# Score matmuls issued as four column tiles of 32 keys, in two softmax attention layers

## The chip, the cores and the metric

The kernel runs on one NeuronCore of a Trainium2 chip. The metric is the device time of one execution in microseconds. The kernel before takes 2621.23 us, the median of three runs (2619.69 to 2622.96).

Five engines run side by side and meet at semaphores: TensorE (matmuls; PE in the profile, its weight loads PEld), VectorE (DVE), ScalarE (ACT), GpSimd (POOL) and SyncE (SP, which issues transfers here). A matmul here is always a pair: a load of the stationary operand into TensorE's array, and a matmul that streams the moving operand past it into PSUM. A form such as `64*128` in the profile gives the part of the array that a pair occupies: 64 rows (the contraction) by 128 columns (the output partitions).

## The reference

Four layers follow each other, each added to its input x (2048 tokens, width 512, 32 heads of 16): softmax attention A, linear attention B, then A and B again with the same weights. The change touches only A:

```python
qkv = (x @ wqkv).reshape(B, S, 3, H, Dh)            # after a layer norm
scores = jnp.einsum("bhqd,bhkd->bhqk", q, k) * (Dh ** -0.5)
p = _softmax(scores, axis=-1)
o = jnp.einsum("bhqk,bhkd->bhqd", p, v)
return o.transpose(...).reshape(B, S, D) @ wo
```

## The kernel before

**Staging.** The heads of an A layer are taken in four octets (8 heads) of two groups (4 heads) each, g = 0 to 7. For each group two tiles `kq` of 128 partitions hold keys and queries in fp16. A head takes 64 partitions: 48 rows are the 16 dimensions in three products of high and low fp16 parts, the rest carries the softmax shift. So one `kq` tile holds two heads, one in partitions 0 to 63 (u = 0), one in 64 to 127 (u = 1).

**The loop.** Attention walks through (g, j, kt): group, block of 512 queries (4), tile of 128 keys (16), 8 x 4 x 16 = 512 steps a layer. `scores` (L807) does a step's two halves. A half takes one PSUM tile `s` of two banks (128 partitions x 2 x 512), runs one matmul for each of two heads into it (L813: stationary 64x128 keys, moving 64x512 queries), and one exponential on ScalarE (L816) from `s` to the SBUF tile `p` in float32. The pool `psS` has three such `s` tiles, `pp` has six `p` tiles. Since the two heads lie in different row halves of the array, their matmuls can run at the same time.

`pvs` (L819) does the value side two steps later (LAG = 2): for each of four heads one float32 matmul, stationary v of 128 keys x 32, moving p of 128x512, into partitions 32·hh to 32·hh + 31 of the accumulator `pv` (L831). That is the column grid `128*32`: four tiles side by side. The profile shows each float32 matmul as two load and matmul pairs, so 8 a step. After the 16th key tile `norm` (L474) turns and normalizes the result on VectorE.

**The filler.** The next octet's projections, the value projections, the output projection and the preparation of weights for B are cut into pieces; `pump` (L853) takes one piece after a step whenever a credit allows, 0.345 a step in most of the time, 0.55 once the last octet is ready. A piece of the query and key projection is 4 chunks, each as four column tiles of 32 (`mm_cols`, L549; L553), in the grid of the value matmuls; a piece of the value projection (L630) is 16 matmuls of form `128*128`; the row norms take one matmul (L653).

**Order.** In the attention loop the order on TensorE is the program's own (`manual_schedule` for PE): scores of step n, value matmuls of step n - 2, at times a piece of filler. The other engines are ordered by the framework. Between attention and the next layer lies the stage of layer B (L933 and on; its `gather`, L1060, has the matmuls of L1064).

Of the kernel before, what the change touches and what calls it, by code (L numbers as in the profile page):

```python
# [17 lines left out]
P = 128  # L18
# [25 lines left out]
def mha_hedgehog_stack(ctx, tc, x_in, a_wqkv, a_wo, b_wqkv, b_wphi, b_wo, out, shmin=SHMIN):  # L44
    nc = tc.nc
# [537 lines left out]
    class LayerA:  # L583
# [223 lines left out]
        def scores(self, g, j, kt):  # L807
            for half in range(2):
                s = psS.tile([P, 2, 512], F32, tag="S", name="s")
                for u in range(2):  # L810
                    r = 64 * u
                    t = self.kq[g][half]
                    nc.tensor.matmul(s[:, u, :], t[r:r + 64, 0, kt * P:(kt + 1) * P],  # L813
                                     t[r:r + 64, 1, j * 512:(j + 1) * 512], start=True, stop=True)
                pt = pp.tile([P, 2, 512], F32, tag="p", name="p")
                nc.scalar.activation(pt, s, AF.Exp, scale=0.25 / (QS * QS))  # L816
                self.pt[(g, j, kt, half)] = pt
# [470 lines left out]
```

## Time and profile before

| what | us |
|---|---|
| median of three runs | 2621.23 |
| the profiled execution | 2620.91 |
| its span in the profile | 2619.1 |
| first attention, first to last exponential | 84 to 1080 |
| second attention, first to last exponential | 1391 to 2364 |

Layer B and the preparation of the first layer fill the rest. How to read the lines that follow: a group line has line, engine, operation, output and inputs, form, shapes and count; then busy time, mean duration of one in ns, and the idle time of the engine just before it with what ended it. A timeline line has start (us from the start of the span), length of the merged run, engine, line, operation and count. A line of the chain has start, length, engine, what and line. TensorE's durations are from start to modelled end, so matmuls in a row overlap: the distance of two starts tells their cost.

### The profile page before, as it was taken

How to read it: one execution, taken by the hardware profiler on the slowest of the kernel's cores; microseconds unless marked ns; L12 is line 12 of the kernel's file. 1: busy time of each engine (PE TensorE's matmuls, PEld its weight loads, DVE VectorE, ACT ScalarE, POOL GpSimd, SP SyncE). 2: the span in 40 equal slices, each digit the busy share in tenths (PEclk: the TensorE clock that was granted, in tenths of full speed). 3: DMA queues.
4: the chain of work that ended last, by engine and by line, in shares of the span. 5: the costliest groups of instructions: out<-in, count | busy, mean ns of one | idle time of the engine just before them, and what ended most of it. 6: DMA issues, size and time to landing. Idle time of an engine off the chain costs nothing.

```text
span 2619.1 us, 50234 instructions
## 1 busy us (share of the span) xinstructions
PE 2503.1 (96%) x20960; PEld 812.9 (31%) x20960; DVE 997.4 (38%) x1902; ACT 2196.1 (84%) x2436; POOL 371.5 (14%) x502
## 2 busy tenths in 40 slices
PE   6899999999999899999899999999999999999998
PEld 4322222222223122355343222222222212224543
DVE  6211211221223533689872122112211302338897
ACT  5799999999899899654437999999999999994552
POOL 3000000000000000266430000000000000004552
PEclk8999999999999899999999999999999999999999
DMA  4500220130113411100234003201301230110003
GB/s 147 110 29 9 47 40 5 27 50 11 57 27 84 157 45 46 41 25 1 73 96 67 13 11 51 32 5 28 60 5 26 56 74 32 48 44 26 9 17 106
DMA packets 52414, 120.43 MB, mean 46 GB/s; under 512 B 11024, under 2 KB 14224, under 8 KB 49360
## 3 DMA queue, kind: packets, MB, share of 16 engines
q1 hardware_dynamic: 51504, 114.76, 18.3%
q8 instruction: 166, 2.72, 0.4%
q0 software_dynamic: 672, 2.36, 0.2%
q14 instruction: 72, 0.59, 0.1%
HBM read 60.06 MB, written 31.59 MB: 35 GB/s over the span
## 4 chain that ended last, share of the span: by engine, by line
PE 73%; DVE 12%; ACT 8%; issue 4%; POOL 2%; DMA 1%; ACTq 0%; SPq 0%; POOLq 0%; DVEq 0%
PE pv L831 33%; PE s L813 20%; ACT p L816 6%; PE pqk L553 5%; PE po L553 5%; DVE su L1017 2%; PE pk L946 1%; PE pbv L946 1%; PE pq L946 1%; POOL f L1026 1%; PE pst L419 1%; DVE f L1009 1%; PE pn L1086 1%; DVE su L1018 1%; DVE yt L503 1%
## 5 line engine op out<-in xcount | busy, mean ns | idle before, releaser
L816 ACT ACTIVATE p<-s 128x1024 f32<-128x1024 f32 x2048 | 1907.0, 1075 | 63.9 <-PE s L813 58.0
L831 PE MATMUL pv<-p,v 128*32 128x512 f32 x8192 | 1096.3, 607 | 13.8 <-DVE yt L476 13.7
L813 PE MATMUL s<-kq 64*128 64x512 f16 x4096 | 676.8, 384 | 23.2 <-DMA kq<-sh 2.8
L813 PEld LDWEIGHTS <-kq 64*128 64x128 f16 x4096 | 157.7, 93 | 805.6 <-issue 792.0
L831 PEld LDWEIGHTS pv<-p,v 128*32 128x32 f32 x8192 | 162.4, 108 | 370.9 <-issue 331.6
L645 POOL TENSOR_TENSOR sq<-stg 128x512 bf16<-128x512 f16 x48 | 68.9, 1435 | 1313.0 <-DVE stg L696 1306.1
L695 DVE TENSOR_SCALAR tq<-pqk,c_qk 128x512 f32<-128x512 f32 x48 | 35.1, 732 | 451.3 <-PE pqk L553 451.3
L1026 POOL TENSOR_TENSOR f<-f,su 128x1024 f32<-128x1024 f32 x62 | 120.0, 1935 | 575.7 <-DVE su L1020 547.4
L476 DVE STREAM_TRANSPOSE yt<-pv 128x512 f32<-128x512 f32 x64 | 45.8, 716 | 404.9 <-PE pv L831 404.8
L946 PEld LDWEIGHTS <-xnTa 128*128 128x128 f16 x1152 | 109.6, 98 | 139.8 <-DVE f L1010 14.8
L553 PEld LDWEIGHTS <-wA 128*32 128x32 f16 (+1 forms) x2496 | 86.4, 97 | 149.4 <-issue 100.6
L1011 ACT ACTIVATE f<-f,c_pB 128x1024 f32<-128x1024 f32 x64 | 72.5, 1148 | 38.2 <-DVE f L1010 37.9
L553 PE MATMUL pqk<-xnTb,wA 128*32 128x512 f16 (+1 forms) x1248 | 98.4, 381 | 1.1 <-ACT xnTb L429 1.1
L946 PE MATMUL pbv<-wbv,xnTa 128*128 128x512 f16 x384 | 88.2, 379 | 11.0 <-DVE f L1010 11.0
L553 PE MATMUL po<-woA,ob 128*32 128x512 f16 x1536 | 97.5, 379 | 0.0
L553 PE MATMUL pqk<-xnT,wA 128*32 128x512 f16 (+1 forms) x1224 | 92.4, 379 | 2.7 <-DVE xnT L432 2.2
L1032 ACT ACTIVATE fk<-f 128x1024 f16<-128x1024 f32 x30 | 31.7, 1057 | 74.9 <-POOL f L1026 74.9
L541 DVE SCALAR_TENSOR_TENSOR xt<-po,c_oA,xt 128x512 f32<-128x512 f32 x32 | 23.2, 724 | 183.9 <-PE po L553 183.9
L946 PE MATMUL pq<-wbqk,xnTa 128*128 128x512 f16 x384 | 88.4, 379 | 0.0
L946 PE MATMUL pk<-wbqk,xnTa 128*128 128x512 f16 x384 | 88.4, 379 | 0.0
L1058 ACT ACTIVATE qT<-pqt 128x512 f32<-128x512 f32 x64 | 34.7, 593 | 56.6 <-PE pqt L1057 56.6
L1017 DVE TENSOR_REDUCE su<-f 128x64 f32<-128x1024 f32 x64 | 77.5, 1210 | 9.7 <-ACT f L1011 8.9
(261 smaller groups left out, 1936.8 us busy)
## 6 DMA issues: line engine op xcount, KB each, us to landing
kq<-stg SPq DMA_DIRECT2D x96, 128.0 KB, 5.6
xd<-xt SPq DMA_DIRECT2D x24, 512.0 KB, 2.8
xt<-xd SPq DMA_DIRECT2D x24, 512.0 KB, 3.6
kq<-stg SPq DMA_DIRECT2D x96, 96.0 KB, 4.2
kq<-dC SPq DMA_DIRECT2D x64, 128.0 KB, 3.7
oD<-osp SPq DMA_DIRECT2D x24, 256.0 KB, 2.0
ob<-oD SPq DMA_DIRECT2D x8, 768.0 KB, 5.4
xt<-in_A_x_dram SPq DMA_DIRECT2D x8, 512.0 KB, 3.9
```

The costliest lines, as they stand in the source:

```text
L476: nc.vector.transpose(yt.rearrange("p a b -> p (a b)"), ps)
L553: nc.tensor.matmul(ps[r, :], w[:, r], x, start=(n == 0), stop=(n == 11), skip_group_check=cols)
L645: nc.gpsimd.tensor_tensor(sq, hi, hi, ALU.mult)
L695: nc.vector.tensor_scalar(tq, ps, cqk, CLAMP, op0=ALU.mult, op1=ALU.min)
L813: nc.tensor.matmul(s[:, u, :], t[r:r + 64, 0, kt * P:(kt + 1) * P], t[r:r + 64, 1, j * 512:(j + 1) * 512], start=True, stop=True)
L816: nc.scalar.activation(pt, s, AF.Exp, scale=0.25 / (QS * QS))
L831: nc.tensor.matmul(acc[32 * hh:32 * hh + 32, :], self.oct[o]["v"][:, r:r + 32], pt[:, hh % 2, :], start=(kt == 0), stop=(kt == NT - 1), sk ...
L946: nc.tensor.matmul(dst, xnT[:, a, c, t * P:(t + 1) * P], w(b, c), start=(i == 0 and c == 0), stop=(i == 2 and c == NC4 - 1))
L1011: nc.scalar.activation(f, f, AF.Exp, scale=con["pB"])
L1017: nc.vector.tensor_reduce(su, f[:, r, :], AX.X, ALU.add)
L1026: nc.gpsimd.tensor_tensor(f3, f3, self.part_sums(f3, slice(0, 64), factor), ALU.mult)
L1058: nc.scalar.activation(qT[i][:, :, t * P:(t + 1) * P], pst.rearrange("p (g t) -> p g t", g=4), AF.Copy)
```

## The change

The single score matmul of a head and key tile (64 rows x 128 keys) becomes four of 64 rows x 32 keys, each writing its 32 partitions of the same bank. The four read the same queries as moving operand. Their number goes from 4 to 16 pairs of load and matmul a step; the exponential, the value matmuls, the buffers and the filler stay as they are, and so does the order of the work. The first of the four carries the wait for a free `s` tile, and the last of a half tells ScalarE. On TensorE the program goes from 33,767 to 58,343 instructions (this includes a branch for unusual data that isn't run).

```diff
                 for u in range(2):
                     r = 64 * u
                     t = self.kq[g][half]
-                    nc.tensor.matmul(s[:, u, :], t[r:r + 64, 0, kt * P:(kt + 1) * P],
-                                     t[r:r + 64, 1, j * 512:(j + 1) * 512], start=True, stop=True)
+                    for i in range(4):
+                        k0 = kt * P + 32 * i
+                        nc.tensor.matmul(s[32 * i:32 * i + 32, u, :], t[r:r + 64, 0, k0:k0 + 32],
+                                         t[r:r + 64, 1, j * 512:(j + 1) * 512], start=True, stop=True, skip_group_check=True)
```

## The prediction

> **What bounds the kernel now.** I read the page first: the engines' totals and the chain that ended last.
>
> ```profile
> span 2619.1 us, 50234 instructions
> PE 2503.1 (96%) x20960; PEld 812.9 (31%) x20960; DVE 997.4 (38%) x1902; ACT 2196.1 (84%) x2436; POOL 371.5 (14%) x502
> PE 73%; DVE 12%; ACT 8%; issue 4%; POOL 2%; DMA 1%; ACTq 0%; SPq 0%; POOLq 0%; DVEq 0%
> PE pv L831 33%; PE s L813 20%; ACT p L816 6%; PE pqk L553 5%; PE po L553 5%; DVE su L1017 2%; PE pk L946 1%; PE pbv L946 1%; PE pq L946 1%; POOL f L1026 1%; PE pst L419 1%; DVE f L1009 1%; PE pn L1086 1%; DVE su L1018 1%; DVE yt L503 1%
> L816 ACT ACTIVATE p<-s 128x1024 f32<-128x1024 f32 x2048 | 1907.0, 1075 | 63.9 <-PE s L813 58.0
> L831 PE MATMUL pv<-p,v 128*32 128x512 f32 x8192 | 1096.3, 607 | 13.8 <-DVE yt L476 13.7
> L813 PE MATMUL s<-kq 64*128 64x512 f16 x4096 | 676.8, 384 | 23.2 <-DMA kq<-sh 2.8
> L813 PEld LDWEIGHTS <-kq 64*128 64x128 f16 x4096 | 157.7, 93 | 805.6 <-issue 792.0
> L831 PEld LDWEIGHTS pv<-p,v 128*32 128x32 f32 x8192 | 162.4, 108 | 370.9 <-issue 331.6
> L553 PEld LDWEIGHTS <-wA 128*32 128x32 f16 (+1 forms) x2496 | 86.4, 97 | 149.4 <-issue 100.6
> ```
>
> The reader sees TensorE on 73% of the chain, the value matmuls (L831) and the score matmuls (L813, the changed ones) holding 53% between them. There are 2048 exponentials, so 1024 steps of two halves (4096 score matmuls, four a step). The second view is the chain of waits inside 20 us of the first layer's attention, the third the timeline of the same stretch.
>
> ```profile
> by line: PE pv L831 49.7%; PE s L813 31.0%; PE pqk L553 13.0%; ACT p L816 5.5%; issue 1.6%; PE psn L653 1.2%; ACTq L816 0.1%
> 505.96 0.54 PE s L813 x4
> 506.50 1.00 PE pv L831 x8
> 507.50 0.54 PE s L813 x4
> 508.04 0.99 PE pv L831 x8
> 509.03 0.65 PE s L813 x4
> 509.68 0.99 PE pv L831 x8
> 510.68 0.86 PE pqk L553 x16
> 511.54 0.54 PE s L813 x4
> ```
>
> One cycle is three steps and one piece of projection: 511.54 - 505.96 = 5.58 us, all of it TensorE. ScalarE's own pace is in a timeline row where it runs four exponentials without a break:
>
> ```profile
> 205.06 3.79 ACT L816 ACTIVATE p<-s 128x1024 f32<-128x1024 f32 x4
> ```
>
> (3.79 - 1.075)/3 = 0.905 us each, so six want 5.43 us. The two engines are within 3% of each other; TensorE leads, and its only idle time in the cycle is the 0.65 in place of 0.54: 0.11 us in which the third score pair waits for ScalarE to free a bank. In the last eighth of an attention even that is gone:
>
> ```profile
> 130.00:820.00 690.00, 678.97 (x6012) 179.02 (x6010) 140.10 (x256) 674.29 (x726) 35.27 (x29) 1.00 0.18 32
> 2237.00:2364.00 127.00, 125.31 (x1194) 33.50 (x1196) 44.21 (x118) 120.27 (x129) 0.00 (x0) 1.00 0.12 41
> ```
>
> These are windows (columns: window, length, then busy time of PE, PEld, DVE, ACT, POOL, then granted clock, DMA share, GB/s). The second has 129 exponentials in 127 us, 1.97 us a step, with TensorE busy 98.7%.
>
> **The change part by part.** It removes 4 weight loads and 4 matmuls of 64x128 a step and issues 16 and 16 of 64x32: 24 more instructions a step, 24,576 in all. Bytes, banks and ScalarE's work stay. No wait is added: the first of a half's eight waits for the bank, the last one releases ScalarE. Instructions are fetched by queues of their own, the larger of them:
>
> ```profile
> q8 instruction: 166, 2.72, 0.4%
> ```
>
> Even doubled that is 0.8% of the DMA engines, and I cost it at nothing; what covers it is the engines' idle share.
>
> What could be won is the drain between column grids. The timeline shows it:
>
> ```profile
> 504.03 1.06 PE L831 MATMUL pv<-p,v 128*32 128x512 f32 x8
> 504.92 1.05 PE L553 MATMUL pqk<-xnT,wA 128*32 128x512 f16 x16
> 505.90 0.60 PE L813 MATMUL s<-kq 64*128 64x512 f16 x4
> 506.43 1.07 PE L831 MATMUL pv<-p,v 128*32 128x512 f32 x8
> 507.43 0.13 PEld L813 LDWEIGHTS <-kq 64*128 64x128 f16 x4 [0.84 <-issue]
> 507.43 0.61 PE L813 MATMUL s<-kq 64*128 64x512 f16 x4
> ```
>
> From pv to a projection in the same 128*32 grid 0.89 us go by; from pv to scores 507.43 - 506.43 = 1.00: **0.11 us lost** entering the score shape. A score pair streams twice 0.216 (0.60 less its last 0.384), yet 0.53 pass until pv: **0.10 us lost** leaving it. Both are paid in every step, 0.21 us. The first score matmul starts with its load (both rows 507.43), so the load itself isn't on the path; a 64x32 load isn't in the trace, but 64x128 takes 0.093 and 128x32 takes 0.097 to 0.108, and I cost the exchange at nothing.
>
> Does a common column grid remove them? The score tiles keep 64 rows, pv has 128. The trace has a change of rows alone, 128*128 to 64*128:
>
> ```profile
> L630 PE MATMUL pv__619<-wAv,xnT x48: 219/219/219, 51.4 to 54.1; 128*128 128x128 f16 x48
> 105.81 0.67 PE L630 MATMUL pv__1202<-wAv,xnT 128*128 128x128 f16 x9
> 106.41 0.60 PE L813 MATMUL s<-kq 64*128 64x512 f16 x4
> ```
>
> Undisturbed, these follow each other every 2.7/47 = 0.057 us; nine take 0.51, and the scores come 0.60 after the first: 0.09 us lost with the columns unchanged. So a change of rows pays the same drain, and I keep both drains: saving 0. The other bound is both gone, 0.21 a step; it is a rival below.
>
> The Trainium skill (TensorEngine Tiling (Array Packing), Key Properties) says that changing the tiling mode, not just the tile, drains TensorE, and lists 64x32 and 128x32 as different modes; by it too the saving is 0, also where this trace has no row for that very pair.
>
> What is added is the stagger. Tiles of a group start one behind the other, and a drain waits for the last. The two row tiles of a score pair start together: the x4 row is 0.60 = 0.216 + 0.384. For column tiles:
>
> ```profile
> 506.43 0.16 PEld L831 LDWEIGHTS pv<-p,v 128*32 128x32 f32 x8 [0.42 <-issue]
> 504.49 0.12 PEld L553 LDWEIGHTS <-wA 128*32 128x32 f16 x4 [0.30 <-issue]
> ```
>
> Eight loads of 0.108 lie within 0.16, so the last starts 0.05 after the first; four of 0.097 within 0.12, so 0.02 for three gaps, 7 ns each. The eight tiles of a score half therefore end between 0 (as the row tiles do) and 0.05 us later than now. I take 0.035, nearer the column row, since four of each eight are column neighbours and one of the seven gaps is a change of rows. The first half's stagger hides under its own 0.216 us; the second's stands ahead of the drain: +0.035 us of TensorE a step. The next thing late is pv, and after a projection the exponential of the first half.
>
> By the Trainium skill (TensorE: Matmul & The Clock Gate, Part 3) a pack spans one matmul and about 4 ns for each further tile; by that the eighth would be 0.028 late and the sum below a fifth smaller, near 2641.
>
> How much reaches the end: in a three-step cycle the third pair's 0.11 wait absorbs what that pair's side of the loop adds, as ScalarE sets its end; of three staggers two pass. 896 steps x 0.035 x 2/3 = 21 us. The last eighth of each attention (128 steps together) has no such wait: 128 x 0.035 = 4.5 us. The sum is +25 us on the profiled execution's 2620.9 us (span 2619.1 and 1.8 around it), **2646 us**. That execution stands 0.3 us under the median shown, 2621.2. With a stagger of 0.05 and nothing absorbed it is 1024 x 0.05 = +51, with 0.02 and two thirds +14: the likeliest case's own range is 2630 to 2672.
>
> **Can the instructions be fed?** A step now has 24 TensorE instructions and some 9 of filler: 6012 matmuls in 690 us are 8.7 a us, 17.4 with loads. After it is 24 more in 1.9 us, so 30 a us, 33 ns each. The fastest long stretch of this trace:
>
> ```profile
> 1100.94 0.91 PE L1064 MATMUL kvp<-vt,fk 128*128 128x68 f16 x24
> 1101.78 2.77 PE L553 MATMUL po<-woA,ob 128*32 128x512 f16 x48
> 1104.48 0.61 PE L946 MATMUL pk<-wbqk,xnTa 128*128 128x512 f16 x2
> ```
>
> 72 matmuls with their loads, 144 instructions, in 3.54 us: 25 ns each. That is enough on average, though part of them may have stood in the queue beforehand, and a score pair wants 32 in 0.43 us.
>
> **The rivals.**
>
> *The drains go* (faster). If only the column grid counts, a step loses 0.21 us of TensorE: a cycle needs 5.58 - 0.11 - 0.63 = 4.84, and ScalarE's 5.43 bounds it: 0.15 a cycle at most, 0.13 if a little of the hand-over stays, x 299 cycles = 39 us; the last eighths fall from 1.97 to 1.81, 128 x 0.16 = 20. 2621 - 59 = 2562. For it: the projection in pv's grid pays nothing. Against it: L630 to L813. Chance 0.14. With only one drain gone it is about 2580.
>
> *Eight tiles aren't fed or don't overlap* (much slower). Place: the score pair; it decides from 0.216/8 = 27 ns per load and matmul on, where eight no longer fit under one stream. At the L1064 rows' pace, 0.84/24 = 35 ns, 16 pairs take 0.56 in place of 0.43: +0.13 a step, 1024 x 0.13 = +133, about 2750. At the L553 rows' 2.70/48 = 56 ns, which is also four tiles at a time, 0.90: +0.47, about 3080. For it: no row has eight tiles at once, and none holds this rate for long. Against it: the 25 ns above and eight loads in 0.05 us. Chance 0.22.
>
> *Nothing shows*: a stagger like the row tiles' near 0, or one that the 0.11 wait takes whole; 2616 to 2626. Chance 0.08.
>
> **How the numbers follow.** The forecast has 0.56. A difference of 0.2%, 5 us, is about what a measurement of this kernel can tell from none. Faster 0.14 (the drains), same 0.08, slower 0.56 + 0.22 = 0.78. The range takes in the forecast, the case without effect, nearly all of the fast case and the mild end of the unfed one: 2555 to 2745; left out are its worse part, about 0.17, and some 0.03 else.
>
> **What would show it.** Right: the score group has form 64*32, x16384, its eight starts lie within 0.02 to 0.05 us, the chain's score piece grows from 0.54 to 0.56-0.59, and pv to scores keeps 1.00. Wrong: score piece near 0.43 and pv to scores at 0.89 (the drains are gone, and ScalarE runs at 0.905 throughout); or a score piece of 0.67 and more, with loads 30 ns apart (unfed); or a third pair that still waits 0.11 and a cycle of 5.58 (no effect).

## The result and the profile after

The changed kernel takes 2637.65 us, the median of four runs (2636.79 to 2638.74), beside 2621.31 for the kernel before on the same chip (2619.69 to 2622.96, four runs). The ratio is 1.0063, with a 95% interval of 1.0045 to 1.0080: slower by 16.3 us. The forecast was 2646.

The page of the changed kernel (span, engines, the instruction queue, then the groups of the exponential and of the score matmul with its load):

```profile
span 2635.0 us, 74813 instructions
PE 2518.4 (96%) x33248; PEld 840.1 (32%) x33248; DVE 997.1 (38%) x1902; ACT 2199.9 (83%) x2436; POOL 371.1 (14%) x502
q8 instruction: 262, 4.29, 0.7%
L818 ACT ACTIVATE p<-s 128x1024 f32<-128x1024 f32 x2048 | 1910.8, 1075 | 78.9 <-PE s L815 73.4
L815 PE MATMUL s<-kq 64*32 64x512 f16 x16384 | 700.8, 384 | 20.1 <-DMA kq<-sh 5.2
L815 PEld LDWEIGHTS <-kq 64*32 64x32 f16 x16384 | 188.6, 89 | 805.4 <-issue 794.1
```

The score group has its new form, 64*32, sixteen a step, and each matmul still takes 384 ns. TensorE is busy 15 us longer, and the exponential's idle time that scores end has gone from 58.0 to 73.4 us, also 15. The instruction queue went from 0.4 to 0.7%, below the 0.8% allowed for.

The chain of waits in the stretch of the first attention that the prediction read:

```profile
511.30 0.56 PE s L815 x16
511.85 1.00 PE pv L833 x8
512.85 0.56 PE s L815 x16
...
514.40 0.69 PE s L815 x16
...
516.08 0.86 PE pqk L553 x16
516.94 0.56 PE s L815 x16
```

A score piece went from 0.54 to 0.56, and the third one, with its wait for a bank, from 0.65 to 0.69. Values and projection kept 1.00 and 0.86. The cycle is 516.94 - 511.30 = 5.64 us, 0.06 more than the 5.58 before. That this is three times 0.02 is chance: by the experiments below, two of the three go into the third pair's wait, and a later start of ScalarE adds the rest.

The timeline of the same stretch:

```profile
511.22 0.14 PEld L815 LDWEIGHTS <-kq 64*32 64x32 f16 x16 [0.42 <-issue]
511.23 0.63 PE L815 MATMUL s<-kq 64*32 64x512 f16 x16
511.78 1.07 PE L833 MATMUL pv<-p,v 128*32 128x512 f32 x8
512.78 0.62 PE L815 MATMUL s<-kq 64*32 64x512 f16 x16
516.87 0.41 PE L815 MATMUL s<-kq 64*32 64x512 f16 x8
```

The last row is one half alone: eight matmuls end 0.41 us after the first one starts, 0.02 more than the 0.386 of one. That is the stagger; in the trace's starts the eight lie within 23 to 24 ns, 3.3 ns a tile, where the two of before lie within 3 to 4. From values to scores it is 512.78 - 511.78 = 1.00, as before: the drain is still there. From scores to values it is 511.78 - 511.23 = 0.55, before 0.53: that drain stands too, with the stagger ahead of it.

One more change shows where ScalarE waits. In the second attention there is a place where it has idled 1.37 us and then starts on a fresh half. Before, and after:

```profile
1849.47 0.61 PE L813 MATMUL s<-kq 64*128 64x512 f16 x4
1849.97 3.77 ACT L816 ACTIVATE p<-s 128x1024 f32<-128x1024 f32 x4 [1.37 <-PE s L813]
```

```profile
1861.13 0.63 PE L815 MATMUL s<-kq 64*32 64x512 f16 x16
1861.67 2.86 ACT L818 ACTIVATE p<-s 128x1024 f32<-128x1024 f32 x3 [1.37 <-PE s L815]
```

From the first score matmul's start to the exponential's start, the hand-over from here on, it was 0.50 and is 0.54. Over all starts at which ScalarE waited, the medians are 0.491 and 0.541: 50 ns, of which the stagger is 20. The other 30 pass between the last matmul's end and the exponential: 101 ns before, 132 after. The ends of matmuls are modelled, so the trace's semaphore entries say it better: the signal to ScalarE comes 405 ns after the start of a half's last matmul before and 435 after the change, and the exponential starts 83 ns behind the signal in both. So these 30 ns pass on TensorE's side. The prediction has no term for them.

From the start of the first exponential to that of the last the two attentions take 994.2 and 971.7 us before, 1004.2 and 978.1 after: 10.0 + 6.4 = 16.4 us, all of the difference.

### The profile page after: what moved, and what is told of

Read it like the earlier page. It is cut to its first block, busy times and chain, and to the rows that moved or that the text cites. A ratio compares the mean times of both kernels' runs of the same rounds, so it can differ in the third digit from the quotient of the medians.

```text
span 2635.0 us, 74813 instructions
## 1 busy us (share of the span) xinstructions
PE 2518.4 (96%) x33248; PEld 840.1 (32%) x33248; DVE 997.1 (38%) x1902; ACT 2199.9 (83%) x2436; POOL 371.1 (14%) x502
## 4 chain that ended last, share of the span: by engine, by line
PE 73%; DVE 12%; ACT 7%; issue 4%; POOL 2%; DMA 1%; SPq 1%; ACTq 0%; POOLq 0%; DVEq 0%
PE pv L833 33%; PE s L815 21%; ACT p L818 6%; PE pqk L553 5%; PE po L553 5%; DVE su L1019 1%; PE pk L948 1%; PE pbv L948 1%; PE pq L948 1%; POOL f L1028 1%; PE pst L419 1%; DVE st L362 1%; DVE f L1011 1%; DVE su L1020 1%; DVE f L1012 1%
## 5 line engine op out<-in xcount | busy, mean ns | idle before, releaser
L818 ACT ACTIVATE p<-s 128x1024 f32<-128x1024 f32 x2048 | 1910.8, 1075 | 78.9 <-PE s L815 73.4
L815 PE MATMUL s<-kq 64*32 64x512 f16 x16384 | 700.8, 384 | 20.1 <-DMA kq<-sh 5.2
L815 PEld LDWEIGHTS <-kq 64*32 64x32 f16 x16384 | 188.6, 89 | 805.4 <-issue 794.1
```

What stands on the lines that cost most here:

```text
L815: nc.tensor.matmul(s[32 * i:32 * i + 32, u, :], t[r:r + 64, 0, k0:k0 + 32], t[r:r + 64, 1, j * 512:(j + 1) * 512], start=True, stop=True, ...
```

## The experiments

The theory: both drains (the time lost between two matmuls of different form) stay; eight tiles cost TensorE 20 ns a step ahead of a drain, and a half's hand-over to ScalarE comes later. The rivals: the number of instructions is what costs; the order of the tiles is; the drain comes from the column grid after all.

**Half the tiles** (two of 64 keys):

```diff
-                    nc.tensor.matmul(s[:, u, :], t[r:r + 64, 0, kt * P:(kt + 1) * P], ...
+                    for i in range(2):
+                        k0 = kt * P + 64 * i
+                        nc.tensor.matmul(s[64 * i:64 * i + 64, u, :], t[r:r + 64, 0, k0:k0 + 64], ...
```

> Two column tiles of 64 keys in place of four of 32: four tiles a half, 16 instructions a step in place of 8. Theory A: three gaps of 3.3 ns put the last start 10 ns after the first, 6.5 more than before, a third of the changed kernel's 20: +5 us, 2624 to 2629, drains unchanged. Rival: if the 32-column grid itself costs something, nothing shows here, 2621 within 2; if loading 64 columns in place of 128 is slow, the first score after a drain comes later than 0.525 us.

2633.42 us, ratio 1.0051 [1.0037, 1.0064]: +12, where a third of the stagger was expected to cost 5. The view of the score line (duration ns min/median/max, first and last start) and its hand-over at the same place:

```profile
L815 PEld LDWEIGHTS <-kq x8192: 102/103/162, 78.6 to 2373.0; 64*64 64x64 f16 x200
L815 PE MATMUL s<-kq x8192: 372/400/633, 83.1 to 2373.2; 64*64 64x512 f16 x200
```

```profile
1858.09 0.63 PE L815 MATMUL s<-kq 64*64 64x512 f16 x8
1858.62 1.94 ACT L818 ACTIVATE p<-s 128x1024 f32<-128x1024 f32 x2 [1.37 <-PE s L815]
```

The four starts lie within 10 ns, less than half of 23. But a load of 64 columns takes 103 ns, where 128 take 93 and 32 take 89, and the median matmul 400 instead of 386; the second half starts 240 ns after the first instead of 226. These 14 ns make up what the stagger saves: first score to first value is 0.536 us before, 0.556 here and with four tiles. The two kernels cost TensorE the same; the hand-over differs, 0.522 here and 0.541 with four, and so does the time, by 4 us.

**The same number of instructions without column tiles** (each matmul cut into four by 128 queries; 64*128 stays):

```diff
+                for i in range(4):
+                    for u in range(2):
+                        q0 = j * 512 + 128 * i
+                        nc.tensor.matmul(s[:, u, 128 * i:128 * i + 128], t[r:r + 64, 0, kt * P:(kt + 1) * P],
+                                         t[r:r + 64, 1, q0:q0 + 128], ...
```

> The kernel before with each score matmul cut along the queries: four of 64x128 keys by 128 queries, so as many score instructions as in the changed kernel (16 loads, 16 matmuls a step), yet one tile form and no eight-tile stagger. 128 columns follow each other every 56 ns (the L630 row), 4 x 56 = 223 in place of 216, so a half ends 7 to 10 ns later than before. Theory A: a third to a half of the changed kernel's 20 ns, +4 to +8 us, 2625 to 2629; the last score start to pv takes 0.15 (0.305 less 0.16 of shorter streaming). Rival B (the number of instructions costs): +16 us or more, 2637 and up.

2626.51 us, ratio 1.0024 [1.0015, 1.0033]: +6 with the same 16 pairs a step. The count explains 6 us at most, and even these have another reason: the pieces here cost TensorE 15 ns a step (0.551 from first score to first value), while completion is not later (102 ns from the last end to the exponential, 101 before). The row again:

```profile
1853.01 0.62 PE L815 MATMUL s<-kq 64*128 64x128 f16 x16
1853.51 1.94 ACT L818 ACTIVATE p<-s 128x1024 f32<-128x1024 f32 x2 [1.37 <-PE s L815]
```

0.50, as before the change. That the instructions can't be fed is out too: sixteen pairs take 0.62 us here, the four of before 0.61.

**Time on TensorE alone, before the change** (a matmul of 48 queries repeated, once at the end of the second half, once in the first):

```diff
+                    if half == 1 and u == 1:
+                        nc.tensor.matmul(s[:, u, 0:48], t[r:r + 64, 0, kt * P:(kt + 1) * P],
+                                         t[r:r + 64, 1, j * 512:j * 512 + 48], ...
```

> The kernel before, with one more matmul a step: the last score matmul's first 48 query columns are computed once more, 48/512 of 0.213 us = 20 ns of streaming ahead of the drain, two instructions a step in place of 24. Theory A (what counts is the time at which the last score matmul ends): +20 ns of TensorE a step as in the changed kernel, +14 to +20 us, 2635 to 2641. Rival B (the number of instructions costs): a twelfth of the changed kernel's +16, so 2621 to 2624.

> As the run that repeated 48 columns after the second half's last score matmul, but after the first half's: 20 to 23 ns ahead of the first half's end, and since the second half's second matmul sits in the same rows, ahead of the second half's end too. Theory A with the hand-over (a cycle pays what delays the half after the filler and what delays the drain before it, so the delay of one half passes once, of both twice): twice the +8 of the other run in the cycles, +14 to +18 us, 2635 to 2639, as in the changed kernel. Rival (only the time ahead of the drain counts): +8 again, 2629.

In the second half: 2629.08 us, ratio 1.0033 [1.0021, 1.0045]. In the first (`half == 0`): 2629.64, 1.0035 [1.0021, 1.0048]. The chain of the former (L816 is the repeat):

```profile
508.39 0.54 PE s L813 x4
508.93 0.02 PE s L816
...
511.50 0.61 PE s L813 x4
512.11 0.02 PE s L816
...
513.99 0.54 PE s L813 x4
```

From a step's first score to its first value 0.536 us have become 0.558. So 22 ns of TensorE ahead of the drain, about the stagger's amount, cost 8 us, not the 14 to 20 that I expected. The cycle is 5.60, one step's 0.02 more than before and not three: the third pair's piece is 0.61 + 0.02 where it was 0.65, so its wait has taken in the other two. The exponential's hand-over is unchanged there (0.491). The repeat in the first half delays it too, by 18 ns (0.509), and adds 22 to 25 ns of TensorE; I expected more than for the other, and it is the same within the intervals. Its cycle is 5.60 as well:

```profile
506.38 0.86 PE pqk L553 x16
...
511.98 0.86 PE pqk L553 x16
```

The traces show why. Each has 74 cycles of exactly three steps between two whole pieces of projection, and in them one chain goes round: a projection's start to the first score behind it (977 to 979 ns, medians), the hand-over of that half, three exponentials in a row (2855), the `s` tile that they free to the third pair's second half, which waits for it (51), that half to its first value, and from there to the next projection (882 or 883). Two of these stretches differ between the runs:

| run | hand-over behind the projection, ns | third pair's second half to first value, ns | cycle, ns |
|---|---|---|---|
| before | 491 | 322 | 5580 |
| repeat in the second half | 491 | 345 | 5603 |
| repeat in the first half | 509 | 322 | 5599 |
| quartered queries | 499 | 330 | 5597 |
| half the tiles | 522 | 340 | 5627 |
| the change | 541 | 340 | 5647 |

Within 2 ns each cycle grows by what these two grow. What a step adds on TensorE ahead of the third pair's wait is absorbed by it. So in the cycle the repeat in the second half delays TensorE alone and the repeat in the first half the hand-over alone, and either passes whole. Of the change's 67 ns a cycle 50 are the later hand-over and 18 the stagger of one half.

**The order of the tiles** (tile by tile, the two heads in turn):

```diff
+                for i in range(4):
+                    for u in range(2):
+                        k0 = kt * P + 32 * i
```

> The changed kernel with its eight tiles of a half in another order: the two heads (row halves) inside, the four column tiles outside. Theory A (the number of tiles that start one behind the other, and that finish, counts): the last start again some 23 ns after the first, ScalarE again 0.54 us after the first score matmul, 2635 to 2640. If a step from one column tile to the next is dearer than one from one row half to the other, or the reverse, the spread moves: alternating heads with row steps free would halve it to 12 ns, and the time to 2630.

2637.47 us, ratio 1.0065 [1.0051, 1.0079], the changed kernel's time. The order doesn't matter; the hand-over is 0.54 here too.

**Which part of the form drains.** In two kernels the value matmuls use only the first 64 of a tile's 128 keys, which leaves out half of their contraction, so that scores and values have the same rows. In one the scores are those of the change (all forms 64*32), in the other those of before (64*128 beside 64*32).

```diff
-                nc.tensor.matmul(acc[32 * hh:32 * hh + 32, :], self.oct[o]["v"][:, r:r + 32],
-                                 pt[:, hh % 2, :], ...
+                nc.tensor.matmul(acc[32 * hh:32 * hh + 32, :], self.oct[o]["v"][0:64, r:r + 32],
+                                 pt[0:64, hh % 2, :], ...
```

> The changed kernel with value matmuls that use the first 64 keys of each key tile alone (128*32 becomes 64*32; the other half of the contraction is left out, the streamed columns stay). Theory A (a drain follows any change of tile form, rows or columns): scores and values now have one form, 64*32, both drains go, from pv to scores 0.52 us from the last pv start becomes 0.41, from scores to pv 0.31 becomes about 0.20; a step loses 0.2 us of TensorE, ScalarE's 0.905 us bounds it, total 2560 to 2585. Theory C (the column grid alone decides, and what is seen in the changed kernel has another cause): nothing to win by rows, 2638 within 5.

> The kernel before with the same halved value matmuls: scores 64*128, values 64*32, so the rows agree and the columns don't (half of the contraction is left out). Theory A: both drains stay, 0.525 and 0.305 us, total 2621 within 8. If 64-row value matmuls were cheaper for a reason of their own, this run would show it: a gain like that of the run above, 40 us or more, with the drains in place.

With the change: 2620.19 us (median of ten, 2614.78 to 2631.05), ratio 1.0002 [0.9990, 1.0015]. Without it: 2732.71 (of four, 2716.33 to 2750.71), ratio 1.0452 [1.0420, 1.0483]. Both times miss what was expected, the first by 35 us and the second by over 100; the drains themselves are as theory A has them. The first one's timeline:

```profile
503.02 1.05 PE L553 MATMUL pqk<-xnT,wA 128*32 128x512 f16 x16
504.00 0.63 PE L815 MATMUL s<-kq 64*32 64x512 f16 x16
504.44 0.60 PE L833 MATMUL pv<-p,v 64*32 64x512 f32 x4
504.60 0.40 PE L815 MATMUL s<-kq 64*32 64x512 f16 x4
504.87 0.60 PE L833 MATMUL pv<-p,v 64*32 64x512 f32 x4
505.30 0.73 PE L815 MATMUL s<-kq 64*32 64x512 f16 x12
```

Scores to values take 504.44 - 504.00 = 0.44 instead of 0.55: with the whole form equal this drain is gone. Values to scores take 505.30 - 504.87 = 0.43, the values' own pace (504.87 - 504.44), so that one is gone too. The type isn't what drains: scores are fp16 and values float32 here. From the projection (128*32) to scores (64*32), where rows alone change, it is 504.00 - 503.02 = 0.98, as in the changed kernel: that one stands. In the other kernel, where columns alone differ:

```profile
503.04 1.06 PE L831 MATMUL pv<-p,v 64*32 64x512 f32 x8
504.04 1.05 PE L553 MATMUL pqk<-xnT,wA 128*32 128x512 f16 x16
505.02 0.61 PE L813 MATMUL s<-kq 64*128 64x512 f16 x4
505.55 1.06 PE L831 MATMUL pv<-p,v 64*32 64x512 f32 x8
```

Scores to values 0.53, as before: columns alone drain. Values to projection 1.00 instead of the 0.89 that the prediction read: rows alone drain, in the same column grid, for 0.11. Either part of the form is enough, so the change, which makes one of two equal, takes no drain away.

The chain of the first one shows what such a gain is worth:

```profile
503.09 0.98 PE pqk L553 x16
...
506.37 1.04 ACT p L818
...
508.70 0.98 PE pqk L553 x16
```

TensorE has shed five of a cycle's six drains, some 0.5 us, against 0.12 added at the projection, and yet the cycle is 508.70 - 503.09 = 5.61, at a granted clock of 1.00 in this stretch: an exponential of 1.04 now stands in the chain, since the scores wait for an `s` tile. The time falls by 17 us below the changed kernel's. This run isn't a clean price of the drains, because some scores now also pass the values (last section).

The second one's time is not that of its drains. The windows of the first attention (window, length, busy time of PE, PEld, DVE, ACT, POOL, granted clock, DMA share, GB/s), before and here:

```profile
130.00:1075.00 945.00, 920.37 (x8172) 243.21 (x8170) 244.97 (x542) 906.77 (x974) 36.67 (x34) 0.99 0.19 46
```

```profile
130.00:1075.00 945.00, 920.07 (x7500) 220.41 (x7496) 217.25 (x464) 845.75 (x904) 36.59 (x34) 0.92 0.18 42
```

904 exponentials in place of 974, at a granted clock of 0.92. The projection's new drain, 0.11 in each of 299 cycles, is 33 us. In the second attention, at a clock of 0.99, this profiled execution (2716.33 us) is 17 us longer than before from first to last exponential, about half of the 33. In the first it is 81 us longer: the other half, and some 66 for the clock, an estimate that takes 0.07 of 945 us as lost. The four runs have mean clocks of 0.945 to 0.959, the longest the lowest; before it was 0.988 to 0.990.

**Finer filler.** If TensorE's long piece between two steps is what ScalarE waits on, pieces of half the size at twice the rate should win.

```diff
-                    yield from self.project(o, j, ps, ten, 4)
+                    yield from self.project(o, j, ps, ten, 2, True)
...
-                    rate = 0.55 if self.ready == 3 else 0.38 if n < FILLED else 0.345
+                    rate = 0.55 if self.ready == 3 else 0.66 if n < FILLED else 0.6
```

> The kernel before with the projection filler cut into pieces of two chunks (8 matmuls, 0.43 us) in place of four (0.86 us), given out at 0.6 a step in place of 0.345. Theory L (the score half that follows a piece of filler comes too late for ScalarE, and so both engines idle once a cycle): with half the piece the half comes 0.43 us earlier, ScalarE no longer idles, the third pair's wait for it goes too, a three-step cycle falls from 5.58 towards TensorE's own 5.47: 2588 to 2605. Rival (TensorE's sum alone sets the cycle): 2621 within 5.

> The changed kernel with the same finer filler. Theory A with L: with no wait left in the cycle, the stagger of every step passes instead of two in three, so the distance to the run with the kernel before's scores is 1024 x 0.020 = 20 us, against 16 with the coarse filler; 2608 to 2625. If the stagger is hidden once the hand-over is loose, the distance falls to 5 or less.

With the scores of before 2619.47 us, ratio 0.9993 [0.9984, 1.0002]: nothing. With those of the change 2628.70, 1.0031 [1.0018, 1.0043]: the change costs 9 us there, where I expected 20. Why it is less stays open. The chain of the former shows steps that follow faster, and a place where time is lost:

```profile
503.12 0.43 PE pqk L553 x8
...
506.79 0.43 PE pqk L553 x8
...
509.23 0.76 DVE tq L695
...
511.17 0.64 DVE yt L476
...
511.85 1.07 PE pv L832 x8
```

Two steps and a half piece take 506.79 - 503.12 = 3.67 us, 1.83 a step, where the long piece made 5.58/3 = 1.86, though with less filler in it (half a piece in two steps, not one in three). And where an accumulator ends, VectorE is still at a projection's three results (511.17 - 509.23 = 1.9 us) when it should empty the accumulator (yt), and the value matmuls wait. In the view of waits these places are few: without the longest one they come to 6 us here, 4 in the kernel before. So, no piece in the step before such a turn (`near`), two pieces at it:

```diff
-                    if credit >= 1 or turn:
+                    fine = self.ready < 3
+                    if turn and fine:
+                        credit -= 2
+                        self.pump(2)
+                    elif turn or credit >= 1 and not (near and fine):
```

> The finer filler on the kernel before, with no piece given out in the step ahead of an accumulator's turn and two pieces at the turn itself, so that VectorE isn't busy with a projection when it has to empty the accumulator. Theory L (the cycle is the loop of both engines through the filler; the finer pieces shorten it, and what they won was given back at the turns, where value matmuls waited some 40 us for VectorE): 2590 to 2610. Rival (the finer filler wins nothing that isn't lost elsewhere): 2617 to 2622.

2607.11 us (2606.72 to 2607.76), ratio 0.9948 [0.9935, 0.9962]: faster than both kernels, with the scores of before. A turn in its chain (511.53, two pieces in a row), with no work of VectorE in it:

```profile
511.53 0.86 PE pqk L553 x16
```

The values' waits for VectorE at the turns, without the longest, are down to 0.2 us, which is a part of the 14 us won. No run kept the long pieces away from the turns, so how much the size of a piece wins and how much its place isn't shown.

**Fewer drains by longer groups.** Three halves of scores, then the values of three halves (first kernel), or three halves and then one or two whole steps of values (second), instead of two halves and one step. The edit of the first, which has the finer filler too:

```diff
-                    self.scores(g, j, kt)
-                    pend.append((g, j, kt))
+                    for half in range(2):
+                        self.scores(g, j, kt, (half,))
+                        group.append((g, j, kt, half))
+                        if (2 * kt + half) % 3 == 2 or 2 * kt + half == 2 * NT - 1:
...
+                            for h in pend:
+                                self.pvs(*h)
+                            pend, group = group, []
```

> The kernel before with the finer filler and the order on TensorE regrouped: three score halves in a row, then the value matmuls of the three halves before them, so two drains in 1.5 steps in place of two in one. Theory A (the drains are real TensorE time, 0.2 us a step): 0.07 us a step less, TensorE then needs 5.26 us for what ScalarE needs 5.43 for, ScalarE becomes the bound: 2560 to 2585. Rival: the third half waits for ScalarE longer than the drains save, and nothing is won over the finer filler alone, or up to 60 us are lost at the turns of the accumulator.

> The kernel before with the order on TensorE regrouped so that value matmuls stay in whole steps: three score halves, values of two steps, three score halves, values of one step and the filler piece; two changes of form each way in three steps where there were three. Theory A (each change of form is 0.10 us of TensorE): a three-step cycle loses 0.2 us of TensorE time, 5.26 needed, ScalarE's 5.43 bounds it: 2575 to 2595. Rival: the groups make ScalarE wait at other places (two steps of values take 1.9 us, longer than two exponentials), and it is 2621 or slower.

Both are slower. The first takes 2798.05 us, ratio 1.0676 [1.0661, 1.0691], by its own design: the values of one half fill two of the four column tiles, so those of three halves take more than 1.5 steps' 1.49:

```profile
506.71 1.84 PE pv L832 x12
```

The second mends that and has a third fewer drains (four in three steps instead of six): 2638.62 us, ratio 1.0068 [1.0054, 1.0081], where I expected 2575 to 2595.

```profile
504.46 0.54 PE s L813 x4
...
505.02 0.39 PE s L813 x2
505.41 1.85 PE pv L831 x16
```

Its waits say why: the scores, which waited 2.5 us for ScalarE in the run of before, wait 82 here. The view counts only where TensorE stood idle by its modelled ends, so the 0.11 us of each cycle before isn't in the 2.5.

```profile
PE s L813 <- ACT p L816: 82.0, 236, 0.8
```

Three halves at once want three `s` tiles at once, and ScalarE has not freed the last.

## Why the prediction was right, and where only by its sum

**Both drains stay: right.** Values to scores kept 1.00, scores to values kept 0.53 plus the stagger. The argument from the rows (L630 to L813) named the cause, and the two kernels with 64 rows showed it: rows alone drain and columns alone drain. The Trainium skill's rule (TensorEngine Tiling (Array Packing), Key Properties), that a new tiling mode drains TensorE, holds for every pair that was run: 0.09 to 0.11 us where either part differs, none where both agree.

**Fed and overlapped: right.** Sixteen pairs keep the score piece at 0.56, the loads are done in 0.14 us for sixteen. The rival at 2750 to 3080, to which I gave 0.22, has no sign in the trace. (Its upper end was a slip: 1024 x 0.47 is 481, so about 3100.)

**The stagger: right in kind, 20 ns a step against the 35 taken.** I took 5 ns a gap, going mostly by the column row's 7. That is the gap of the float32 value matmuls: four of them start within 20 ns, with 128 rows and, in the kernels with half the contraction, with 64. The fp16 projections behind them without a drain have it too. Behind a drain, in those two kernels, the same projections start within 10 ns, 3.3 a gap, as the fp16 scores do. The Trainium skill (TensorE: Matmul & The Clock Gate, Part 3) has about 4 ns for each further tile, which was the better figure: an estimate by it is seven times 4, 28 ns, and by 3.3 it is 23.

**Two of three staggers pass: wrong, it is one.** The prediction let the third pair's wait absorb what that pair's side of the loop adds. But this wait is ahead of the third pair's second half: it absorbs the staggers of the first two pairs, and the third pair's, which comes behind it, passes. With the repeat in the second half the third pair's wait shrank and one of three shares passed, 23 ns a cycle; over the whole kernel 8 of a possible 1024 x 0.022 = 22.5 us. In the changed kernel the wait looks untouched (0.69 less 0.56) because ScalarE, which ends it, was itself started 50 ns later by the first half after the projection. That wait is a place in a loop through both engines: `s` tile freed, scores, values, projection, scores, exponentials, `s` tile.

**The term that was missing.** A half's hand-over to ScalarE comes 50 ns later, and behind a projection all of it passes into the cycle. The prediction said that an exponential after a projection would be late, but only by the stagger, and its sum has no such term; the last matmul's end to the exponential also went from 101 to 112 to 132 ns with two, four and eight tiles a half. The Trainium skill (TensorE: Matmul & The Clock Gate, Part 3, "The cost: per-tile semaphore tail") puts 4.7 ns on each tile of a group whose end is signalled; an estimate by it is 28 ns from two to eight tiles, and 9 from two to four, where the runs have 31 and 11. The prediction didn't use this rule.

**The sum.** +25 forecast, +16 measured. In a cycle the forecast was 0.070 us, two staggers of 0.035; measured are 0.067, a hand-over of 0.050 and one stagger of 0.018. That these agree is luck: too large a stagger and too large a share stood in for a term left out. The 9 us between the two sums lie in how often a cycle's growth counts. Had all 299 cycles of the prediction's count grown as the 74 did, the change would cost 20 us, and the two repeats, the quartered queries and half the tiles 7, 6, 5 and 14; measured are 16, and 8, 9, 6 and 12. So the loop gives the whole kernel's time to within 4 us, and what happens outside its plain cycles stays open. The last eighth of each attention, which was forecast to add 4.5 us in all, adds 2.0 (125.3 and 125.5 us before, 126.3 and 126.5 after, exponential to exponential). The lower end of the likeliest case's range, 2630, was a slip as well: its +14 gives 2635.

**The price of the rival with the drains gone was not tested.** 2562 took ScalarE's 5.43 as the next bound. The kernel that sheds five of six drains has 5.61, and takes 2620. But two drains stand in the loop, from the projection to the scores and from the third pair to its values; that kernel sheds the second, keeps the first and adds one ahead of the projection. Longer groups saved drains and lost. The loop of three `s` tiles, not the sum of an engine's work, sets the cycle here, so TensorE's time counts where it stands in that loop.

## What to carry to other kernels

A drain is saved only where the whole form, rows and columns, agrees on both sides; compare the forms of both neighbours before reordering or cutting a matmul for it. Count the tiles of a group twice: once as a stagger, and once as a later completion for the engine that waits for the group. A wait absorbs what is added ahead of it, not what is added behind it, and moves when the engine that ends it starts later. Where two engines hand tiles round, ask what a shorter piece releases and who is then waiting; here a filler cut into halves, kept away from the accumulator's turn, won 14 us where no change to the scores did.

## What the hardware showed beyond the question

- A load of 64 columns takes 103 ns, longer than one of 128 (93) or 32 (89), and the matmuls behind it start 14 ns later.
- With values of 64 rows the granted clock fell, to 0.959 over the run with the scores of before (0.988 before) and to 0.979 with those of the change (0.991 after it), though half of the values' contraction was left out. Why is open.
- In the kernel whose forms are all 64*32, four score matmuls (504.60 in its timeline) start between the values' first and last four. By the semaphore entries in the trace these are the last four of their half, those of the second head in rows 64 to 127; they carry the half's signal to ScalarE, and the first head's four start only at 505.30. So matmuls in free rows passed those that wait in other rows, values and the first head's scores alike. In the trace of the changed kernel, where the values take all 128 rows, every half's eight start in the program's order. The signal did not pass: in this place it comes at 505.75, 435 ns after the last of the first head's four, as in the changed kernel. So it is in 622 of the 637 halves in which four passed, and in none does a signal come 435 ns after the passing four. So even here a signal on the last matmul of a group said that the group was done.
